# One VectorE addition moved ahead of a product of a later unit, and the last half tile given a PSUM bank and an output buffer of its own

## The chip, the cores and the metric

The kernel runs on one core of a Trainium2 chip. The metric is the device time of one execution in microseconds (us). The runs of the kernel before lie within 0.7% of each other; what is compared below is the median of several runs, and one execution recorded by the hardware profiler.

Engines are named as the profile names them: PE (TensorE matmuls), PEld (TensorE weight loads), DVE (VectorE), ACT (ScalarE), POOL (GpSimd), SP (the engine that issues many of the transfers). A "q" behind an engine name is that engine's sequencer issuing a DMA or waiting.

## The reference

Linear attention with a decaying state (per batch and head a 48x48 state), then a multiplicative feed-forward block. B=4 batches, H=8 heads, S=768 steps, D=48; 3072 tokens of 384 features, d_ff=1024.

```python
def _attn_ref(r, k, v, w, u):
    state = zeros((B, H, D, D)); y = zeros_like(r)
    for t in range(S):
        kt, vt, rt, wt = k[:, :, t], v[:, :, t], r[:, :, t], w[:, :, t]
        cur = einsum('bhd,bhe->bhde', u[None] * kt, vt)
        y[:, :, t] = einsum('bhd,bhde->bhe', rt, state + cur)
        state = wt[:, :, :, None] * state + einsum('bhd,bhe->bhde', kt, vt)
    return y

def _moe_ref(x, w1, w2, w3, w_out):      # x: y as [3072, 384]
    a = x @ w1
    b = x @ w2
    return (a * b @ w3) @ w_out
```

All inputs and the output are float32; inside, the matmul operands are bf16.

## The kernel before

**Tiles.** The 768 steps are cut into 6 chunks of C=128. A *unit* is one chunk of one or two batches; there are 13 (`UNITS`: chunk, first batch, number of batches). From unit 3 on each has two batches, so its tiles are 128 time steps by 768 values (two batches, 8 heads, 48 features).

**One unit t, attention part.** `ln_t` takes the logarithm of the decay on ACT; `cs_t` forms its running sum with a triangular matmul into two PSUM banks; `e_t`, `ne_t`, `pc_t` (ACT) take exponentials of that sum. `KRk_t`, `rw_t`, `KRr_t` scale k and r; DMA transposes on SP (`dtk_t`, `dtr_t`; PE transposes in early units) turn them. `m_t_b` are the score matmuls, which are masked (`msk` on DVE, or `mcp` on ACT with `maff` on POOL or DVE). `ys_t` and `yi_t_b` sum the state's part and the chunk's own part of y in PSUM. The diagonal term with u goes beside it: `rk_t` (r times k), `ruk_t` (times u), `dg_t` (sum over a head), `dv_t` (times v). `yb_t` (L627) adds the PSUM y and `dv_t` into a bf16 tile in SBUF, on DVE. Unit 7 then transposes that tile on PE (`yt_7`, L646) and copies it to `xT` (`xT_7`, L650); units 6 and 8 to 12 do this by DMA transposes (`dty_t_b`, L636).

**One unit t, feed-forward part** (`block`). `a_t_g` and `b_t_g` (L727) are the two products x w1 and x w2 in 4 groups, `asb_t_g` copies a to SBUF on ACT, `abT_t_g` multiplies it with b out of PSUM on DVE. `o_t_b` (L748) multiplies with w34, the product of w3 and w_out that was formed earlier, eight matmuls for a tile of 128 tokens by 384 columns; `osb_t_b` (L753) copies the bank to an output buffer and `st_t_b` (L757) stores it. The tile (11, 0) is the last one (`LAST`); it is computed in two halves of 192 columns, `o_11_0` and `oh_11_0`, with two copies (`osb_11_0` on DVE, `osbh_11_0` on ACT) and two stores (`st_11_0` from SP, `sth_11_0` from ACT).

**What sets the order.** Each step registers a function under its name; `ORDER` is one long list of `step@engine` that is issued in this order, so every engine works through its own steps in the order of the list. PSUM has 8 banks; `BANKS` gives by name which bank (or pair) a step uses, and which of a few SBUF buffers (`so11_0=1` is output buffer 1 for tile (11, 0)). `one(key)` is the view of a bank. Waits are derived from these: a step that writes a bank waits for the last reader of that bank, and a reader waits for the last write to the bank that is issued ahead of it. So `cs10=3,4` and `y7=3,4` say that `cs_10` on PE has to wait until `yb_7` has read the y of unit 7 out of banks 3 and 4.

`rk` and the other work tiles are doubled (`N_A = 2`), so unit 10 uses the buffer that unit 8 used. The loads of r, k, v and w are issued from POOL and SP far ahead; late units land in tiles that held weights (`w_bf`, `wo_bf` in the profile's names).

Of the kernel before, what the change touches and what calls it, by code (L numbers as in the profile page):

```python
# [59 lines left out]
a10_3=6 b10_3=1 sa10_3=2 o10_0=1 so10_0=3 o10_1=1 so10_1=1 cs11=0,1 m11_0=4,5 M11_0=1 m11_1=0,1 M11_1=3 y11=2,3  # L60
a11_0=5 b11_0=4 sa11_0=1 a11_1=4 b11_1=1 sa11_1=1 a11_2=2 b11_2=6 sa11_2=2 a11_3=0 b11_3=7 sa11_3=0 o11_0=2 so11_0=1
o11_1=3 so11_1=0 cs12=5,6 m12_0=5,6 M12_0=0 m12_1=0,1 M12_1=2 y12=1,2 a12_0=5 b12_0=7 sa12_0=0 a12_1=1 b12_1=4
sa12_1=1 a12_2=3 b12_2=2 sa12_2=2 a12_3=6 b12_3=5 sa12_3=2 o12_0=4 so12_0=3 o12_1=0 so12_1=2
"""
ORDER = """
table@ACT zeros@DVE mask1@DVE win_0@POOL kin_0@SP ones@DVE win_2@POOL rin_0@SP u@SP padkr@DVE padr@DVE vin_0@SP
# [36 lines left out]
asb_5_3@ACT b_5_1@PE S_7@POOL osb_4_0@ACT abT_5_3@DVE m_7_0@PE st_4_0@SP ys_7@PE ruk_7@POOL mcp_7_0@ACT m_7_1@PE  # L103
abT_5_1@DVE st_2_1@SP kv_8@PE msk_7_1@DVE st_2_0@SP a_6_2@PE dtk_8@SP cs_9@PE maff_7_0@POOL dg_7@DVE b_6_0@PE ne_9@ACT
dtr_8@SP T_8@DVE a_6_0@PE asb_6_2@ACT KRk_9@DVE e_9@ACT yi_7_0@PE a_6_3@PE rw_9@DVE dtk_9@SP dv_7@DVE asb_6_0@ACT
yi_7_1@PE o_4_1@PE ln_10@ACT rk_10@DVE win_11@SP yb_7@DVE KRr_9@POOL o_5_0@PE osb_4_1@ACT dg_8@DVE Sb_7@ACT pc_9@ACT
asb_6_3@ACT cs_10@PE rk_9@DVE dtr_9@SP yt_7@PE ruk_9@POOL e_10@ACT o_5_1@PE xT_7@DVE st_4_1@SP osb_5_0@DVE pc_10@ACT
ne_10@ACT abT_6_0@DVE b_6_2@PE dv_8@POOL iw_10@ACT osb_5_1@DVE b_6_3@PE abT_6_2@DVE st_5_1@SP ln_12@ACT m_8_0@PE
abT_6_3@DVE m_8_1@PE rin_12@POOL ys_8@PE mcp_8_1@ACT a_7_2@PE dg_9@DVE a_6_1@PE rin_11@POOL asb_7_2@ACT msk_8_0@DVE
# [28 lines left out]
def kernel(  # L138
# [13 lines left out]
    nc = tc.nc  # L152
    B, H, S, D = r.shape
    C = 128
# [16 lines left out]
    def many(n, shape, dt, name):  # L171
        return [sb.tile(shape, dt, name=f"{name}_{i}", tag=f"{name}_{i}") for i in range(n)]
# [28 lines left out]
    osb = many(N_OSB, [P, DM], F32, "osb")  # L201
# [25 lines left out]
    bank = {}  # L227
    for e in BANKS.split():
        key, _, at = e.partition("=")
# [3 lines left out]
    def op(name):  # L233
        def keep(fn):
            assert name not in steps, name
            steps[name] = fn
            return fn
        return keep

    def copier(eng):  # L240
        return {"ACT": nc.scalar.copy, "DVE": nc.vector.tensor_copy, "POOL": nc.gpsimd.tensor_copy}[eng]
# [4 lines left out]
    def one(key):  # L246
        return banks[:, bank[key], :]
# [74 lines left out]
    QUEUE = {"SP": nc.sync, "POOL": nc.gpsimd, "ACT": nc.scalar}  # L322
# [26 lines left out]
    for h in range(N_W12):  # L349
        f = slice(h * (DFF // N_W12), (h + 1) * (DFF // N_W12))  # L350
# [13 lines left out]
    for h in range(N_W3):  # L364
        f = slice(h * FI // N_W3, (h + 1) * FI // N_W3)
# [345 lines left out]
    def block(t):  # L711
        c, b0, nb = UNITS[t]
        T = nb * C
        per = 512 // T
        x, ab = xT[t % N_X], abT[t % N_AB]
        for g in range(FI // per):
            def gv(z):
                return one(f"{z}{t}_{g}").rearrange("p (f t) -> p f t", t=T)

            for z, wt in (("a", w1_bf), ("b", w2_bf)):  # L720
                @op(f"{z}_{t}_{g}")
                def _(eng, z=z, wt=wt, g=g, gv=gv):
                    o = one(f"{z}{t}_{g}").rearrange("p (f t) -> p f t", t=T)
                    for f in range(per):
                        fi = g * per + f
                        for di in range(DI):
                            nc.tensor.matmul(o[:, f, :], lhsT=wt[:, di, fi * P:(fi + 1) * P], rhs=x[:, di, :T],  # L727
                                             start=(di == 0), stop=(di == DI - 1))

            @op(f"asb_{t}_{g}")  # L730
            def _(eng, g=g):
                copier(eng)(a_sb[bank[f"sa{t}_{g}"]], one(f"a{t}_{g}"))  # L732

            @op(f"abT_{t}_{g}")
            def _(eng, g=g):
                sa = a_sb[bank[f"sa{t}_{g}"]]
                nc.vector.tensor_mul(ab[:, g * per:(g + 1) * per, :T], sa.rearrange("p (f t) -> p f t", t=T),  # L737
                                     one(f"b{t}_{g}").rearrange("p (f t) -> p f t", t=T))
        for b in range(nb):
            row = (b0 + b) * S + c * C  # L740
            parts = 2 if (t, b) == LAST else 1
            for z, mark in enumerate(("", "h")[:parts]):
                cols = slice(z * DM // parts, (z + 1) * DM // parts)

                @op(f"o{mark}_{t}_{b}")
                def _(eng, b=b, cols=cols):
                    for fi in range(FI):
                        nc.tensor.matmul(one(f"o{t}_{b}")[:, cols], lhsT=ab[:, fi, b * C:(b + 1) * C],  # L748
                                         rhs=w34[:, fi, cols], start=(fi == 0), stop=(fi == FI - 1))

                @op(f"osb{mark}_{t}_{b}")
                def _(eng, b=b, cols=cols):
                    copier(eng)(osb[bank[f"so{t}_{b}"]][:, cols], one(f"o{t}_{b}")[:, cols])  # L753

                @op(f"st{mark}_{t}_{b}")
                def _(eng, row=row, b=b, cols=cols):
                    QUEUE[eng].dma_start(out[row:row + C, cols], osb[bank[f"so{t}_{b}"]][:, cols])  # L757

    for fi in range(FI):
        w34_block(fi)  # L760
# [6 lines left out]
    with tc.manual_schedule():  # L767
        for e in ORDER.split():
            name, _, eng = e.partition("@")
# [37 lines left out]
```

## Time and profile before

| | |
|---|---|
| median of 3 runs | 164.16 us (163.75, 164.16, 164.83) |
| profiled execution, its own time | 163.85 us |
| its span | 162.1 us (1.75 us lie around it) |
| mean granted TensorE clock | 0.997 |
| PE / DVE / ACT / POOL busy | 153.5 / 125.4 / 96.9 / 103.2 us |
| DMA | 25.83 MB in 103,718 packets |

The span runs from the first to the last recorded instruction. A row of the timeline gives start, duration, engine, line, operation, output and inputs, shapes, and how many instructions are merged in it; in square brackets stands how long the engine sat idle before and what released it. The starts of instructions that follow each other on DVE or ACT lie some 0.08 us ahead of the end of the one before, and those of matmuls some 0.16 us: durations include the pipeline. So the pace of a chain of matmuls is read from start to start.

### The profile page before, as it was taken

The numbers are of one execution on the slowest core, as the hardware profiler recorded it, in microseconds if no ns is written. First come the engines' busy times: TensorE is split into PE (matmuls) and PEld (weight loads), VectorE is DVE, ScalarE is ACT, GpSimd is POOL, SyncE is SP. The second block draws the span as 40 slices with busy tenths as digits, with TensorE's granted clock in tenths as the row PEclk, the third lists the DMA queues.
The fourth block names the chain that finished last, engine by engine and source line by source line (L and its number), as shares of the span: only waits on it lengthen the run. The fifth ranks groups of instructions, "written<-read, shape, count | busy, mean of one in ns | idle before, by whom it ended". The sixth has DMA issues, their size and how long they took to land.

```text
span 162.1 us, 4606 instructions
## 1 busy us (share of the span) xinstructions
PE 153.5 (95%) x1923; PEld 117.3 (72%) x1923; DVE 125.4 (77%) x201; ACT 96.9 (60%) x161; POOL 103.2 (64%) x96
## 2 busy tenths in 40 slices
PE   6878899999999999999999989999999999999991
PEld 2336489977767699678887858877778678988760
DVE  6299977728997899999888999999696964566600
ACT  3157842575299598784988759579456544433230
POOL 7997996855268798799697539978628673000000
PEclk9999999999999999999999999999999999999998
DMA  6999999999999999999999997999998925132042
GB/s 111 222 159 180 196 195 242 209 170 215 219 155 161 177 259 167 137 120 172 147 186 169 230 202 195 94 142 132 184 174 182 201 28 146 28 121 97 6 146 97
DMA packets 103718, 25.83 MB, mean 159 GB/s; under 512 B 95825, under 2 KB 101713, under 8 KB 103697
## 3 DMA queue, kind: packets, MB, share of 16 engines
q0 software_dynamic: 76096, 15.18, 115.3%
q1 hardware_dynamic: 27456, 10.26, 30.5%
q8 instruction: 15, 0.25, 0.7%
q10 hardware_dynamic: 144, 0.10, 0.2%
q14 instruction: 7, 0.05, 0.1%
HBM read 27.98 MB, written 4.72 MB: 202 GB/s over the span
## 4 chain that ended last, share of the span: by engine, by line
PE 62%; DMA 20%; POOL 6%; DVE 6%; issue 2%; SPq 1%; ACT 0%; DVEq 0%; POOLq 0%
PE banks L727 31%; PE banks L748 18%; DMA rin<-in_r_dram 9%; DMA w_bf<-in_moe_w_dram 8%; DMA u_f<-in_u_dram 4%; PE banks L564 3%; PE banks L609 2%; PE banks L437 1%; PE banks L680 1%; PE banks L599 1%; PE banks L525 1%; POOL w_bf L358 1%; DVE dg L543 1%; POOL win L343 1%; POOL kin L343 1%
## 5 line engine op out<-in xcount | busy, mean ns | idle before, releaser
L727 PE MATMUL banks<-xT,w_bf 128*128 128x256 bf16 (+1 forms) x624 | 68.6, 264 | 0.0
L727 PEld LDWEIGHTS <-w_bf 128*128 128x128 bf16 x624 | 55.5, 98 | 7.0
L737 DVE TENSOR_TENSOR abT<-a_sb,banks 128x512 bf16<-128x512 f32 x48 | 31.9, 683 | 17.1 <-ACT a_sb L732 9.6
L732 ACT COPY a_sb<-banks 128x512 f32<-128x512 f32 x48 | 27.6, 591 | 21.5 <-PE banks L727 14.7
L748 PE MATMUL banks<-w,abT 128*128 128x384 bf16 (+1 forms) x200 | 33.9, 320 | 0.0
L748 PEld LDWEIGHTS <-abT 128*128 128x128 bf16 x200 | 18.8, 98 | 10.4
L583 DVE TENSOR_TENSOR Mbf<-banks,mask 128x1024 bf16<-128x1024 f32 x14 | 16.9, 1216 | 0.8 <-PE banks L564 0.6
L753 ACT COPY osb<-banks 128x384 f32<-128x384 f32 (+1 forms) x18 | 8.5, 471 | 13.6 <-PE banks L748 11.8
L421 ACT ACTIVATE lw<-win 128x768 bf16<-128x768 f32 (+1 forms) x13 | 10.3, 799 | 10.3 <-DMA win<-in_w_dram 10.3
L343 POOL DMA_DIRECT2D win<-in_w_dram x11 | 12.5, 1140 | 2.8 <-DMA wo_bf<-in_moe_w_out_dram 1.3
L537 POOL TENSOR_TENSOR ruk<-rk,u_bc 128x768 bf16<-128x768 bf16 (+1 forms) x7 | 10.8, 1537 | 4.9 <-DVE rk L533 4.4
L627 DVE TENSOR_TENSOR yb<-banks,dv 128x768 bf16<-128x768 f32 (+1 forms) x13 | 11.6, 892 | 2.4 <-PE banks L609 1.7
L570 ACT CAST Mbf<-banks 128x1024 bf16<-128x1024 f32 x10 | 10.0, 1014 | 4.6 <-PE banks L564 4.5
L454 ACT ACTIVATE NEt<-banks 128x768 bf16<-128x768 f32 (+1 forms) x13 | 9.9, 768 | 3.8 <-PE banks L437 2.7
L343 POOL DMA_DIRECT2D kin<-in_k_dram x8 | 9.1, 1143 | 4.5 <-issue 3.2
L543 DVE TENSOR_REDUCE dg<-ruk 128x16 f32<-128x768 bf16 (+1 forms) x13 | 11.5, 881 | 0.1
L316 PE MATMUL banks<-zeros 128*128 128x512 bf16 x35 | 10.0, 428 | 1.3 <-DVE zeros L257 1.3
L343 POOL DMA_DIRECT2D rin<-in_r_dram x8 | 9.1, 1142 | 2.3 <-PE banks L564 1.4
L343 POOL DMA_DIRECT2D vin<-in_v_dram x8 | 9.1, 1140 | 0.4 <-DMA rin<-in_r_dram 0.4
L564 PE MATMUL banks<-KRT 64*128 64x128 bf16 x192 | 8.1, 217 | 0.4 <-ACT KRT L529 0.3
L609 PEld LDWEIGHTS <-Mbf 128*128 128x128 bf16 x192 | 6.8, 96 | 1.9 <-DVE Mbf L583 0.7
L564 PEld LDWEIGHTS <-KRT 64*128 64x128 bf16 x192 | 5.5, 94 | 3.4 <-issue 1.1
(103 smaller groups left out, 243.6 us busy)
## 6 DMA issues: line engine op xcount, KB each, us to landing
out_dram<-osb SPq DMA_DIRECT2D x23, 192.0 KB, 2.3
win<-in_w_dram POOLq DMA_DIRECT2D x9, 384.0 KB, 10.1
w_bf<-in_moe_w_dram POOLq DMA_DIRECT2D x4, 512.0 KB, 12.6
w_bf<-in_moe_w_dram POOLq DMA_DIRECT2D x4, 384.0 KB, 8.3
rin<-in_r_dram POOLq DMA_DIRECT2D x7, 192.0 KB, 10.1
kin<-in_k_dram POOLq DMA_DIRECT2D x7, 192.0 KB, 10.0
vin<-in_v_dram POOLq DMA_DIRECT2D x7, 192.0 KB, 9.1
wo_bf<-in_moe_w_out_dram POOLq DMA_DIRECT2D x1, 768.0 KB, 11.3
```

The source lines that it names most:

```text
L343: QUEUE[eng].dma_start(dst, src)
L421: nc.scalar.activation(LW[:, :, :D], ww, Act.Ln)
L537: vec(eng).tensor_mul(ruks.rearrange("t (b h) d -> t b (h d)", b=nb), rks.rearrange("t (b h) d -> t b (h d)", b=nb), u_bc[:, None, :].to_b ...
L543: nc.vector.reduce_sum(dgs, ruks, axis=AX.X)
L564: nc.tensor.matmul(o[:, e, q, :], lhsT=KRTs[a:a + PAD, 0, b * HP + q, :], rhs=KRTs[a:a + PAD, 1, b * HP + q, :], start=True, stop=True)
L583: nc.vector.tensor_mul(Mbf[bank[f"M{t}_{b}"]], mview(), mask.rearrange("s (j q) t -> s j q t", j=2))
L609: nc.tensor.matmul(o[:, h % 2, b, h // 2, :], lhsT=M[:, h % 2, h // 2, :], rhs=vv[:, b * H + h, :], start=(not c and b == 0 and h < 2), st ...
L627: nc.vector.tensor_add(ybs.rearrange("t b (q e d) -> t e (b q) d", e=2, d=D), yview().rearrange("t e (x d) -> t e x d", d=D), dvs.rearrang ...
L727: nc.tensor.matmul(o[:, f, :], lhsT=wt[:, di, fi * P:(fi + 1) * P], rhs=x[:, di, :T], start=(di == 0), stop=(di == DI - 1))
L732: copier(eng)(a_sb[bank[f"sa{t}_{g}"]], one(f"a{t}_{g}"))
L737: nc.vector.tensor_mul(ab[:, g * per:(g + 1) * per, :T], sa.rearrange("p (f t) -> p f t", t=T), one(f"b{t}_{g}").rearrange("p (f t) -> p f ...
L748: nc.tensor.matmul(one(f"o{t}_{b}")[:, cols], lhsT=ab[:, fi, b * C:(b + 1) * C], rhs=w34[:, fi, cols], start=(fi == 0), stop=(fi == FI - 1))
```

## The change

Two edits. In `ORDER`, `yb_7@DVE` and `rk_10@DVE` change places (`win_11@SP`, a load of w for unit 11, stands between them and keeps its place on SP). In `block`, the second half of the last tile gets keys of its own, `oh11_0` for the bank and `soh11_0` for the output buffer: PSUM bank 6 in place of bank 2, and output buffer 0 in place of buffer 1. Engines, instructions, shapes and the number of instructions stay the same.

```diff
-sa12_1=1 a12_2=3 b12_2=2 ... o12_0=4 so12_0=3 o12_1=0 so12_1=2
+sa12_1=1 a12_2=3 b12_2=2 ... o12_0=4 so12_0=3 o12_1=0 so12_1=2 oh11_0=6 soh11_0=0
...
-yi_7_1@PE o_4_1@PE ln_10@ACT rk_10@DVE win_11@SP yb_7@DVE KRr_9@POOL o_5_0@PE ...
+yi_7_1@PE o_4_1@PE ln_10@ACT yb_7@DVE win_11@SP rk_10@DVE KRr_9@POOL o_5_0@PE ...
...
                 @op(f"o{mark}_{t}_{b}")
-                def _(eng, b=b, cols=cols):
+                def _(eng, b=b, cols=cols, mark=mark):
                     for fi in range(FI):
-                        nc.tensor.matmul(one(f"o{t}_{b}")[:, cols], lhsT=ab[:, fi, b * C:(b + 1) * C],
+                        nc.tensor.matmul(one(f"o{mark}{t}_{b}")[:, cols], lhsT=ab[:, fi, b * C:(b + 1) * C],
...
                 @op(f"osb{mark}_{t}_{b}")
-                    copier(eng)(osb[bank[f"so{t}_{b}"]][:, cols], one(f"o{t}_{b}")[:, cols])
+                    copier(eng)(osb[bank[f"so{mark}{t}_{b}"]][:, cols], one(f"o{mark}{t}_{b}")[:, cols])
...
                 @op(f"st{mark}_{t}_{b}")
-                    QUEUE[eng].dma_start(out[row:row + C, cols], osb[bank[f"so{t}_{b}"]][:, cols])
+                    QUEUE[eng].dma_start(out[row:row + C, cols], osb[bank[f"so{mark}{t}_{b}"]][:, cols])
```

On DVE, in the stretch where units 7 to 10 overlap, the instructions stand like this; `yb_111` is the y tile of odd units (here `yb_7`), `rk_102` the r k tile of even units (here `rk_10`), `dv_109` the diagonal term of unit 7, `dg_106` that of unit 8, and the last row is `rk_9`. The names in square brackets are the counters that the instruction waits for (DMASW: a load from POOL).

```order
 L491 TENSOR_TENSOR rw_87<-w_bf,iw_85 128x768 [waits DMASW6_49]
 L552 TENSOR_TENSOR dv_109<-vin_73,dg_107 128x768 [waits DMASW5_49,DVE_49]
+L627 TENSOR_TENSOR yb_111<-banks,dv_109 128x2x8x48 [waits DVE_49,PE_49]
 L533 TENSOR_TENSOR rk_102<-w_bf 128x768 [waits DMASW6_49,DMASW0_49]
-L627 TENSOR_TENSOR yb_111<-banks,dv_109 128x2x8x48 [waits DVE_49,PE_49]
 L543 TENSOR_REDUCE dg_106<-ruk_104 128x16
 L533 TENSOR_TENSOR rk_103<-w_bf 128x768
```

The addition moved up by one place, directly behind the product `dv_7` that it reads; nothing else on DVE moved.

On ACT, at the very end of the program, the copies of the last output tiles stand like this; `osb_137` to `osb_140` are the output buffers 0 to 3, the 128x192 rows are `osbh_11_0` and its store `sth_11_0`.

```order
 L753 COPY osb_140<-banks 128x384 [waits DMAHW6_49,DVE_49,PE_49]
 L753 COPY osb_139<-banks 128x384 [waits DMAHW7_49,PE_49]
-L753 COPY osb_138<-banks 128x192 [waits DMAHW0_49,DVE_49]
-L757 DMA out_dram<-osb_138 128x192 [waits Activation_49]
+L753 COPY osb_137<-banks 128x192 [waits DMAHW1_49,PE_49,Activation_49]
+L757 DMA out_dram<-osb_137 128x192 [waits Activation_49]
```

The last copy no longer waits for a DVE instruction but for PE, and for the store that last read output buffer 0 (DMAHW1). On PE the first matmul of `oh_11_0` now waits for ACT, the last reader of bank 6 (`asb_12_3`); on POOL and SP nothing moved.

More of the change, by code (lines that the diff above doesn't have):

```diff
@@ L62 @@
 o11_1=3 so11_1=0 cs12=5,6 m12_0=5,6 M12_0=0 m12_1=0,1 M12_1=2 y12=1,2 a12_0=5 b12_0=7 sa12_0=0 a12_1=1 b12_1=4
-sa12_1=1 a12_2=3 b12_2=2 sa12_2=2 a12_3=6 b12_3=5 sa12_3=2 o12_0=4 so12_0=3 o12_1=0 so12_1=2
+sa12_1=1 a12_2=3 b12_2=2 sa12_2=2 a12_3=6 b12_3=5 sa12_3=2 o12_0=4 so12_0=3 o12_1=0 so12_1=2 oh11_0=6 soh11_0=0
 """
@@ L105 @@
 dtr_8@SP T_8@DVE a_6_0@PE asb_6_2@ACT KRk_9@DVE e_9@ACT yi_7_0@PE a_6_3@PE rw_9@DVE dtk_9@SP dv_7@DVE asb_6_0@ACT
-yi_7_1@PE o_4_1@PE ln_10@ACT rk_10@DVE win_11@SP yb_7@DVE KRr_9@POOL o_5_0@PE osb_4_1@ACT dg_8@DVE Sb_7@ACT pc_9@ACT
+yi_7_1@PE o_4_1@PE ln_10@ACT yb_7@DVE win_11@SP rk_10@DVE KRr_9@POOL o_5_0@PE osb_4_1@ACT dg_8@DVE Sb_7@ACT pc_9@ACT
 asb_6_3@ACT cs_10@PE rk_9@DVE dtr_9@SP yt_7@PE ruk_9@POOL e_10@ACT o_5_1@PE xT_7@DVE st_4_1@SP osb_5_0@DVE pc_10@ACT
@@ L745, in _ @@
                 @op(f"o{mark}_{t}_{b}")
-                def _(eng, b=b, cols=cols):
+                def _(eng, b=b, cols=cols, mark=mark):
                     for fi in range(FI):
-                        nc.tensor.matmul(one(f"o{t}_{b}")[:, cols], lhsT=ab[:, fi, b * C:(b + 1) * C],
+                        nc.tensor.matmul(one(f"o{mark}{t}_{b}")[:, cols], lhsT=ab[:, fi, b * C:(b + 1) * C],
                                          rhs=w34[:, fi, cols], start=(fi == 0), stop=(fi == FI - 1))
                 @op(f"osb{mark}_{t}_{b}")
-                def _(eng, b=b, cols=cols):
-                    copier(eng)(osb[bank[f"so{t}_{b}"]][:, cols], one(f"o{t}_{b}")[:, cols])
+                def _(eng, b=b, cols=cols, mark=mark):
+                    copier(eng)(osb[bank[f"so{mark}{t}_{b}"]][:, cols], one(f"o{mark}{t}_{b}")[:, cols])
                 @op(f"st{mark}_{t}_{b}")
-                def _(eng, row=row, b=b, cols=cols):
-                    QUEUE[eng].dma_start(out[row:row + C, cols], osb[bank[f"so{t}_{b}"]][:, cols])
+                def _(eng, row=row, b=b, cols=cols, mark=mark):
+                    QUEUE[eng].dma_start(out[row:row + C, cols], osb[bank[f"so{mark}{t}_{b}"]][:, cols])
     for fi in range(FI):
```

## The prediction

> **What bounds the kernel now.** I read first the page's busy times and its chain of waits, to see which engine sets the end.
>
> ```profile
> span 162.1 us, 4606 instructions
> PE 153.5 (95%) x1923; PEld 117.3 (72%) x1923; DVE 125.4 (77%) x201; ACT 96.9 (60%) x161; POOL 103.2 (64%) x96
> PE 62%; DMA 20%; POOL 6%; DVE 6%; issue 2%; SPq 1%; ACT 0%; DVEq 0%; POOLq 0%
> ```
>
> PE carries the chain, but 95% is an average. The busy time by stretch shows where PE still has gaps, and PE's own waits between 95.8 and 158.6 us show who makes them.
>
> ```profile
> core 0: us, PE busy (x) PEld busy (x) DVE busy (x) ACT busy (x) POOL busy (x), PEclk, DMA share, GB/s
> 95.90:126.00 30.10, 30.10 (x385) 24.01 (x386) 26.59 (x41) 20.07 (x32) 21.66 (x17) 1.00 1.48 159
> 126.00:158.60 32.60, 32.59 (x341) 25.51 (x339) 18.20 (x27) 12.76 (x21) 6.71 (x6) 1.00 0.44 94
> 158.60:162.10 3.50, 0.00 (x0) 0.00 (x0) 0.36 (x1) 0.32 (x1) 0.00 (x0) 0.88 0.34 112
> PE banks L437 <- DVE yb L627: 0.6, 1, 0.6
> PEld L437 <- DVE yb L627: 1.0, 1, 1.0
> ```
>
> From 95.9 to 158.6 us PE has no gap at all, at full clock; then come 3.5 us in which PE has nothing left. The only wait of PE in this part is for a `yb` at its beginning. So a microsecond saved there moves all later matmuls, as long as nothing else becomes late; and the tail adds directly to the time. The two edits touch just these two places, and I work them out apart.
>
> **Edit 1: `yb_7` ahead of `rk_10`.** PE's timeline at the gap:
>
> ```profile
> 92.50 2.76 PE L748 MATMUL banks<-w,abT 128*128 128x384 bf16 x16
> 95.89 0.50 PE L437 MATMUL banks<-lw,LT 128*128 128x384 bf16 x2 [0.62 <-DVE yb L627]
> 96.43 0.49 PE L646 MATMUL banks<-I,yb 128*128 128x128 bf16 x6
> 96.76 1.46 PE L748 MATMUL banks<-w,abT 128*128 128x384 bf16 x8
> 98.06 0.71 PE L727 MATMUL banks<-xT,w_bf 128*128 128x256 bf16 x5
> ```
>
> The first row is `o_4_1` and `o_5_0`, the second `cs_10`, then `yt_7`, `o_5_1`, `b_6_2`. Eight matmuls of L748 take 1.30 us from start to start (96.76 to 98.06), so sixteen from 92.50 end their turn at 95.10. `cs_10` started at 95.89: the gap is **0.79 us** by this pace (0.62 by the row, which counts the pipeline's tail as busy). `cs_10` writes banks 3 and 4, which `yb_7` reads. On DVE and POOL:
>
> ```profile
> 92.10 0.95 DVE L552 TENSOR_TENSOR dv<-vin,dg 128x768 bf16<-128x768 bf16 x1
> 92.97 2.00 DVE L533 TENSOR_TENSOR rk<-w_bf 128x768 bf16<-128x768 bf16 x1
> 94.89 0.94 DVE L627 TENSOR_TENSOR yb<-banks,dv 128x768 bf16<-128x768 f32 x1
> 95.75 0.94 DVE L543 TENSOR_REDUCE dg<-ruk 128x16 f32<-128x768 bf16 x1
> 96.61 0.54 DVE L533 TENSOR_TENSOR rk<-w_bf 128x768 bf16<-128x768 bf16 x1
> 98.60 0.55 DVE L753 COPY osb<-banks 128x384 f32<-128x384 f32 x1
> 92.39 2.15 POOL L499 TENSOR_TENSOR KR<-rw,Et 128x768 bf16<-128x768 bf16 x1 [1.90 <-ACT Et L495]
> ```
>
> `rk_10` took 2.00 us, while the same product at 96.61 took 0.54. What is different is POOL: `KRr_9` ran until 92.39 + 2.15 = 94.54, and `rk_10` ended at 94.97, 0.43 later, as if it had begun when POOL was done. Is that a rule of this kernel? I looked for other pairs.
>
> ```profile
> 83.12 1.15 DVE L491 TENSOR_TENSOR rw<-w_bf,iw 128x768 bf16<-128x768 bf16 x1
> 83.03 0.82 POOL L702 TENSOR_TENSOR Sst<-Tst,pc 128x384 f32<-128x384 f32 x1
> 105.13 0.95 DVE L627 TENSOR_TENSOR yb<-banks,dv 128x768 bf16<-128x768 f32 x1
> 105.35 1.63 POOL L499 TENSOR_TENSOR KR<-rw,Et 128x768 bf16<-128x768 bf16 x1 [0.39 <-issue]
> 75.01 0.96 DVE L627 TENSOR_TENSOR yb<-banks,dv 128x768 bf16<-128x768 f32 x1 [0.23 <-PE banks L609]
> 75.53 1.49 POOL L552 TENSOR_TENSOR dv<-vin,dg 128x768 bf16<-128x768 bf16 x1
> ```
>
> The product of two SBUF tiles at 83.12 also ended 0.42 us behind POOL's (84.27 against 83.85). But a `yb`, whose first input is in PSUM, takes 0.95 us beside a POOL product (105.13, 75.01), and POOL's are not stretched by it either (1.63 and 1.49). So I take it that `rk` is held by POOL and `yb` is not.
>
> The Trainium skill's page "SBUF — State Buffer", section "SBUF: two separate sides", says that VectorE and GpSimd share one pair of ports as an exclusive lock for a whole instruction, and that VectorE needs it in a two-port mode or with two SBUF inputs. The rows above agree, for both kinds. By the page `yb_7`, with one SBUF input, leaves `KRr_9` alone, and the sum below stands; had one such input been enough for the lock, the third rival's time would come out.
>
> Then the new order gives: `yb_7` starts when `dv_7`, which it reads, is through (92.10 + 0.95 = 93.05), ends at about 94.0; `rk_10` starts behind it, waits for POOL as before, and still ends at about 94.97. `rk_10` pays nothing for its move, since it only loses time that it spent waiting; its reader `ruk_10` stands 14 places behind it on DVE. If the cover were gone (`KRr_9` at 1.63 us as in the row at 105.35, done at 94.0) `rk_10` would end at 94.5, earlier still. DVE goes on with `dg_8` at 94.89 in place of 95.75, **0.86 us** earlier, and with it `rk_9`, `xT_7` and the copy at 98.60.
>
> PE can now start `cs_10` at 95.10, a full microsecond after `yb_7` ended: 0.79 us gained. What is late next? `yt_7` would start at 95.64 and writes bank 2, which ACT must have copied out:
>
> ```profile
> 94.90 0.59 ACT L732 COPY a_sb<-banks 128x512 f32<-128x512 f32 x1
> ```
>
> That ends at 95.49: a margin of 0.15 us. `xT_7` wants `rk_9` out of the way (0.86 earlier) and `yt_7` (0.79 earlier): both come. `m_8_0` needs bank 6, copied out by the row at 98.60, which moves by more than PE does. From here on every engine hands on to the next, so they move together; only what is tied to DMA could stay behind. The closest such place is unit 8's transposes (`dty_8`), with PE beside it:
>
> ```profile
> L636 SPq DMA_TRANSPOSE xT<-yb x2: 1190/1218/1246, 106.1 to 107.3; - x2
> DMA to landing us min/median/max: 4.5/4.9/5.3
> 111.62 2.34 PE L727 MATMUL banks<-xT,w_bf 128*128 128x256 bf16 x20
> 58.52 0.66 PE banks L727 x6
> L636 SPq DMA_TRANSPOSE xT<-yb x12: 1179/1248/2288, 78.2 to 140.6; - x12
> DMA to landing us min/median/max: 2.3/4.7/6.2
> ```
>
> The second transpose is issued at 107.35 and lands 4.5 us later, at 111.86; `a_8_0`, its first reader, follows six matmuls behind 111.62, at 112.28. The margin is 0.4 us. The first transpose follows `yb_8` (105.13 + 0.95) at once, so its issue moves with DVE and PE, by 0.79. I cost this at nothing; if the landing did not move at all, PE would wait 0.79 - 0.42 = 0.37 us and keep 0.42. If it took the 6.2 us of the longest, PE would wait 1.3 us.
>
> **Edit 2: the tail.** The end of the program by the timeline:
>
> ```profile
> 156.79 1.81 PE L748 MATMUL banks<-w,abT 128*128 128x384 bf16 x18
> 158.63 0.36 DVE L753 COPY osb<-banks 128x192 f32<-128x192 f32 x1 [4.66 <-PE banks L748]
> 159.03 0.32 ACT L753 COPY osb<-banks 128x192 f32<-128x192 f32 x1 [1.23 <-DVE osb L753]
> 159.37 0.37 ACTq L757 DMA_DIRECT2D out_dram<-osb  x1
> out_dram<-osb ACTq DMA_DIRECT2D x1, 96.0 KB, 1.7
> out_dram<-osb SPq DMA_DIRECT2D x4, 192.0 KB, 1.9
> ```
>
> PE's last matmul ends at 158.60. Although `o_11_0` was done eight matmuls earlier, its DVE copy starts only at 158.63, since both halves lie in one bank; and the ACT copy of the other half waits for DVE's. Then come the store's issue at 159.37 and 1.7 us to its landing. With a bank of its own the DVE copy goes beside `oh_11_0`, and the ACT copy starts where DVE's did: 159.03 - 158.63 = **0.40 us** gained. The new waits cost nothing that I can find. Bank 6 was last read by `asb_12_3`, without which PE could not have begun `o_12_0`, 24 matmuls ahead. Output buffer 0 was last stored by `st_11_1`, issued when `o_11_1` was copied; from there to PE's end lie two whole tiles and two halves, 2 x 1.30 + 2 x 0.66 = 3.9 us, and a store lands after 1.9 us (last row). Nothing stands behind the ACT copy but its own store. On SP, `st_11_0` now goes out some 0.66 us earlier, into a queue with nothing behind it. Bounds of this term: 0 (if the copy waited for something else) and 0.40.
>
> **The sum**, against the profiled execution: 163.85 - 0.79 - 0.40 = 162.66 us. The median of the runs shown is 0.31 above that execution, so I expect 164.16 - 1.19 = 162.97, **163.0 us**, 0.7% less. All rivals are told on that base. Differences within 1% (1.64 us) are about what a measurement of this kernel cannot tell from no change, so my forecast itself falls there.
>
> **Rivals.**
> - *The first gain is eaten by the transposes.* For it: a margin of 0.4 us, and landings that scatter between 2.3 and 6.2 us. Against it: issue and competing loads move along. With landings that stay where they are PE keeps 0.42, so 163.3; at 1.2 us later than now it keeps nothing, 163.8.
> - *Slower: the same transposes land much later.* Where they take the longest seen, 6.2 in place of 4.5 us, `a_8_0` waits 1.3 us: 164.16 - 1.19 + 1.3 = 164.3, slower than before. It decides from 1.6 us later on; over 1% slower would need 3.2 us, which no transpose here came near.
> - *`yb_7` holds POOL back.* `KRr_9` needed 2.15 us where its like needs 1.63: it seems to have waited 0.5 us at its start, behind `dv_7`. If `yb_7` went ahead of it too, it would end 0.95 us later, `rk_10` at 95.9, and the copy at 98.60 would come 0.1 us later than now and end at 99.25. `m_8_0` on PE, which needs its bank, stood twelve matmuls (1.3 us) behind 98.06, at about 99.4: PE would give back all but some 0.1 us: 163.7. The rows at 75.01 and 105.13 speak against it.
> - *The change does not do what it says*: `cs_10` waits for something else that is late as well. But PE's waits name `yb` alone, and `ln_10`, its input, stands on ACT ahead of the copy at 94.90. 163.8, with the tail alone.
>
> **How the numbers follow.** Forecast 0.62; gain eaten (163.3 to 163.8) 0.17; slower by the transposes 0.06; POOL held back 0.06; no effect at `cs_10` 0.05; the remaining 0.04 for what I do not see. The runs before spread over 1.1 us, so a median may be off by some 0.4 us either way. The range from 162.2 to 164.1 holds the forecast with that spread, and the rivals up to 163.8; 164.3 stays out. Faster by over 1% needs 0.45 us more than the sum, which only the spread gives: 0.18. Slower by over 1%: 0.05. Within 1%: 0.77.
>
> **What would show it.** In the new profile: `yb` at about 93.1 with 0.95 us, `rk_10` behind it still ending at about 95.0; `cs_10` at 95.1 without the wait for `yb`; PE without gaps until about 157.8; the ACT half copy 0.03 us behind PE's last matmul, and a span near 160.9. A PE wait at L727 for a transpose near 111.5 would mean the first rival; a `KRr_9` over 3 us the third. I would be wrong most simply if the matmuls do not run back to back once everything comes 0.8 us earlier.

## The result, and the profile after

| | before | after |
|---|---|---|
| median | 164.16 us (19 runs, 163.39 to 165.35) | 163.0 us (19 runs, 162.42 to 164.28) |
| ratio, 95% interval | | 0.9925 [0.9906, 0.9943] |
| profiled execution | 163.85 us | 164.28 us |
| start of `kv_3` on PE in it | 52.43 | 54.06 |
| from there to PE's last end | 106.17 | 105.37 |
| from PE's last end to the end of the span | 3.50 | 3.14 |

The change is faster by 0.75% with an interval clear of zero: about 1.2 us, as forecast. The profile of the changed kernel must be read with care, though: its execution is the slowest of the 19, even slower than the profiled one of before. The chain of waits says where that comes from: one piece of it (start, duration, what) and PE's row of `kv_3` and `kv_4`, first of before, then of after.

```profile
36.72 13.93 DMA rin<-in_r_dram
52.43 0.69 PE L680 MATMUL banks<-vin,KR 128*64 128x48 bf16 x32
```

```profile
36.70 15.58 DMA rin<-in_r_dram
54.06 0.69 PE L680 MATMUL banks<-vin,KR 128*64 128x48 bf16 x32
```

A load of r for unit 4, issued at the same time in both, landed 1.6 us later, and `kv_3` (L680), which starts 1.78 us behind that landing in both, started 1.63 us late; the work behind it runs late by as much. Neither edit lies ahead of that point. So the starts below are read against it: 1.63 is to be taken off. One of the profiles further down, of the kernel with `KRr_9` on DVE, is from a disturbed execution too (167.14 us, its median 163.74); durations at one place are read from it, and one late transfer, which speaks for that execution alone.

DVE and POOL of after, where the additions and products stand (start, duration, what):

```profile
93.72 0.95 DVE L552 TENSOR_TENSOR dv<-vin,dg 128x768 bf16<-128x768 bf16 x1
94.78 0.96 DVE L627 TENSOR_TENSOR yb<-banks,dv 128x768 bf16<-128x768 f32 x1
95.65 0.94 DVE L533 TENSOR_TENSOR rk<-w_bf 128x768 bf16<-128x768 bf16 x1
96.51 0.94 DVE L543 TENSOR_REDUCE dg<-ruk 128x16 f32<-128x768 bf16 x1
94.02 2.15 POOL L499 TENSOR_TENSOR KR<-rw,Et 128x768 bf16<-128x768 bf16 x1 [1.90 <-ACT Et L495]
```

`yb_7` begins 0.11 us after `dv_7` is through and is not stretched beside POOL. `KRr_9` takes 2.15 us, as before: `yb_7` did not hold it back. `rk_10` now overlaps POOL for only half a microsecond, takes 0.94 us in place of 2.00, and ends at 96.59, 0.42 behind POOL's end, as before (95.0 when 1.63 is taken off). PE at the same place, and its busy time from there on:

```profile
94.13 2.76 PE L748 MATMUL banks<-w,abT 128*128 128x384 bf16 x16
96.72 0.49 PE L437 MATMUL banks<-lw,LT 128*128 128x384 bf16 x2
95.30:158.20 62.90, 62.90 (x722) 49.41 (x721) 46.20 (x69) 33.85 (x57) 29.23 (x23) 1.00 0.98 127
```

`cs_10` starts 2.59 us behind `o_4_1` (3.39 before), the pace of sixteen matmuls, with no wait; and PE is busy for 62.90 of the 62.90 us from 95.30 to 158.20. Unit 8's two transposes, the closest place behind it that hangs on a DMA (the first row ends with their issues, 106.9 and 108.2):

```profile
L636 SPq DMA_TRANSPOSE xT<-yb x2: 1188/1218/1247, 106.9 to 108.2; - x2
DMA to landing us min/median/max: 4.2/4.6/5.0
```

The tail:

```profile
158.80 0.36 DVE L753 COPY osb<-banks 128x192 f32<-128x192 f32 x1 [4.00 <-PE banks L748]
159.51 0.32 ACT L753 COPY osb<-banks 128x192 f32<-128x192 f32 x1 [0.89 <-PE banks L748]
159.85 0.37 ACTq L757 DMA_DIRECT2D out_dram<-osb  x1
```

PE's last matmul ends at 159.43. The DVE copy begins 0.62 us ahead of that, the ACT copy 0.08 behind it (0.43 before).

### The profile page after: what moved, and what is told of

It reads as the page before. It is cut to its first block, busy times and chain, and to the rows that moved or that the text cites. A ratio compares the mean times of both kernels' runs of the same rounds, so it can differ in the third digit from the quotient of the medians.

```text
span 162.6 us, 4604 instructions
## 1 busy us (share of the span) xinstructions
PE 154.0 (95%) x1921; PEld 117.7 (72%) x1923; DVE 124.6 (77%) x201; ACT 97.1 (60%) x161; POOL 103.2 (63%) x96
## 4 chain that ended last, share of the span: by engine, by line
PE 65%; DMA 23%; POOL 6%; issue 2%; ACT 1%; DVE 1%; POOLq 0%; ACTq 0%
PE banks L727 33%; PE banks L748 19%; DMA rin<-in_r_dram 10%; DMA w_bf<-in_moe_w_dram 8%; DMA win<-in_w_dram 5%; PE banks L564 3%; PE banks L609 2%; POOL win L343 2%; POOL kin L343 2%; PE banks L437 1%; PE banks L680 1%; PE banks L599 1%; PE banks L525 1%; POOL rin L343 1%; POOL Mbf L578 1%
## 5 line engine op out<-in xcount | busy, mean ns | idle before, releaser
L727 PE MATMUL banks<-xT,w_bf 128*128 128x256 bf16 (+1 forms) x624 | 68.6, 264 | 0.0
L727 PEld LDWEIGHTS <-w_bf 128*128 128x128 bf16 x624 | 55.5, 98 | 7.0
L316 PE MATMUL banks<-zeros 128*128 128x512 bf16 x33 | 10.6, 462 | 1.3 <-DVE zeros L257 1.2
```

What stands on the lines that cost most here:

```text
L316: nc.tensor.matmul(banks[:, at, :], lhsT=zeros[:, :C], rhs=zeros, start=True, stop=True)
```

## The experiments

The explanation to be tested: two edits, each at its own place, that add up; POOL holds `rk` and not `yb`; PE has no gap behind `cs_10`, so what is saved there stays. Beside the timed ratio, two stretches of each profile are read, since the landing of r at 50 us moves whole executions by more than the effect: from the start of `kv_3` to PE's last end, and from there to the end of the span. Each ratio is against executions of the kernel before that were taken with it; the two stretches are of one profile each.

| kernel | ratio to before, 95% interval | `kv_3` to PE's end | PE's end to the end |
|---|---|---|---|
| before | | 106.17 | 3.50 |
| after | 0.9925 [0.9906, 0.9943] | 105.37 | 3.14 |
| order alone | 0.9960 [0.9946, 0.9975] | 105.36 | 3.49 |
| tail alone | 0.9974 [0.9958, 0.9990] | 106.15 | 3.13 |
| bank alone (one execution) | | 106.16 | 3.11 |
| `yb_7` later still | 1.0065 [1.0041, 1.0089] | 107.02 | 3.51 |
| after, `rk_10` behind `dg_8` | 0.9937 [0.9912, 0.9962] | 105.37 | 3.13 |
| `KRr_9` on DVE, old order | 0.9948 [0.9921, 0.9975] | not read | |
| after, `dv_7` early (one execution) | | 106.00 | 3.15 |
| after, last tile 288 + 96 | 0.9937 [0.9913, 0.9961] | 105.37 | 3.18 |

**The order alone**

```diff
-... ln_10@ACT rk_10@DVE win_11@SP yb_7@DVE KRr_9@POOL ...
+... ln_10@ACT yb_7@DVE win_11@SP rk_10@DVE KRr_9@POOL ...
```

> Only yb_7 and rk_10 change places. Theory (the two edits act apart, each at its own place): PE's 0.79 us gap ahead of cs_10 goes and nothing gives it back, so the time falls by 0.79 us against the kernel before (ratio 0.995); in the profile cs_10 follows o_5_0 without a wait, rk_10 ends when it did relative to KRr_9 (0.43 us behind POOL's end), and the tail still has the DVE copy behind PE's end and the ACT copy 0.40 us behind that. Rival (the order brings less, because part of it is given back later, and the tail carries the gain): under 0.4 us less, with a PE wait of some 0.4 us at a later L727 row.

```profile
93.23 2.76 PE L748 MATMUL banks<-w,abT 128*128 128x384 bf16 x16
95.83 0.49 PE L437 MATMUL banks<-lw,LT 128*128 128x384 bf16 x2
```

0.66 us less by the ratio (0.41 to 0.89), 0.81 in the first stretch and nothing beyond 0.01 in the second. `cs_10` follows `o_4_1` by 2.60 us, and from 90 us on PE has no wait, at `cs_10` or at L727: nothing was given back. The tail is the old one, the DVE copy 0.04 and the ACT copy 0.43 behind PE's end (158.53):

```profile
158.57 0.36 DVE L753 COPY osb<-banks 128x192 f32<-128x192 f32 x1 [4.66 <-PE banks L748]
158.96 0.32 ACT L753 COPY osb<-banks 128x192 f32<-128x192 f32 x1 [1.24 <-DVE osb L753]
```

**The tail alone**

The edits of `BANKS` and `block` stay as in the change; the order goes back to the old one. Against the changed kernel:

```diff
-... ln_10@ACT yb_7@DVE win_11@SP rk_10@DVE KRr_9@POOL ...
+... ln_10@ACT rk_10@DVE win_11@SP yb_7@DVE KRr_9@POOL ...
```

> Only the last half tile gets its own bank and buffer; rk_10 stays ahead of yb_7. Theory: PE's gap at cs_10 stays at 0.79 us by the pace (0.62 by the wait row), the ACT half copy starts within 0.1 us of PE's last matmul in place of 0.44, so the time falls by 0.35 to 0.40 us (ratio 0.998). Rival (the order carries all of the change): no difference, with the end of the program waiting for the other store in place of the ACT copy.

0.43 us less by the ratio (0.16 to 0.69), 0.37 in the second stretch, 0.02 in the first. Its wait at `cs_10` is still there, and the ACT copy starts 0.08 behind PE's end (158.43):

```profile
PE banks L437 <- DVE yb L627: 0.6, 1, 0.6
158.51 0.32 ACT L753 COPY osb<-banks 128x192 f32<-128x192 f32 x1 [0.89 <-PE banks L748]
```

The two stretches of the edits add up to those of both: 0.81 + 0.37 = 1.18 us against 0.80 + 0.36 = 1.16.

**The bank alone, the output buffer shared**

Against the kernel with the tail alone:

```diff
-... oh11_0=6 soh11_0=0
+... oh11_0=6 soh11_0=1
```

> As the tail edit alone, but the half tile keeps output buffer 1 and gets only its own bank. Theory (the shared bank made both copies wait): the DVE copy runs beside the last eight matmuls, the ACT copy starts within 0.1 us of PE's last matmul, as with both. Rival (the shared buffer made the second copy wait): the ACT copy starts 0.4 us behind PE's last matmul, as before. One look, read from the profile's last rows and not from the time.

```profile
158.70 0.36 DVE L753 COPY osb<-banks 128x192 f32<-128x192 f32 x1 [4.00 <-PE banks L748]
159.36 0.32 ACT L753 COPY osb<-banks 128x192 f32<-128x192 f32 x1 [0.84 <-PE banks L748]
```

With PE's end at 159.32 the ACT copy starts 0.04 behind it. In this one execution the bank is the whole of the gain (3.11 us behind PE's end, against 3.13); a buffer of its own adds nothing, and the copy even starts 0.04 later with it. With it the copy also waits for ACT's own earlier copy into buffer 0 and for that buffer's last store; whether one of these is the reason was not tried.

**The addition later still**

```diff
-... ln_10@ACT rk_10@DVE win_11@SP yb_7@DVE KRr_9@POOL o_5_0@PE osb_4_1@ACT dg_8@DVE ...
+... ln_10@ACT rk_10@DVE win_11@SP KRr_9@POOL o_5_0@PE osb_4_1@ACT dg_8@DVE yb_7@DVE ...
```

> The opposite of the order edit: yb_7 goes one place further back, behind dg_8, on the kernel before. Theory (PE waits for yb_7 at cs_10 and for nothing else there, and no later slack takes it up): yb_7 starts 0.86 us later, the wait row at cs_10 grows from 0.62 to about 1.48 us, and the time grows by 0.86 us against the kernel before (ratio 1.005). Rival (later slack takes up a delay): cs_10 late by as much, but the time within 0.3 us of before, with fewer or shorter waits elsewhere on PE.

```profile
97.05 0.50 PE L437 MATMUL banks<-lw,LT 128*128 128x384 bf16 x2 [1.48 <-DVE yb L627]
```

The wait is 1.48 us in place of 0.62, and the first stretch 0.85 longer; by the ratio 0.67 to 1.46 us slower. A delay at `cs_10` goes to the end one for one, and so did the gain.

**`rk_10` behind `dg_8`, on the changed kernel**

```diff
-... yb_7@DVE win_11@SP rk_10@DVE KRr_9@POOL o_5_0@PE osb_4_1@ACT dg_8@DVE ...
+... yb_7@DVE win_11@SP KRr_9@POOL o_5_0@PE osb_4_1@ACT dg_8@DVE rk_10@DVE ...
```

> The changed kernel with rk_10 one place further back, behind dg_8. Theory (rk_10 is held while KRr_9 runs on POOL, yb and dg are not): dg_8 starts right behind yb_7, rk_10 then starts when KRr_9 is done or nearly so and takes 0.55 us to at most 0.7 us in place of 0.94; rk_9 comes some 0.4 us earlier. PE has no gap there any more, so the time is that of the changed kernel (ratio 0.9925 to before, within 0.2%). Rival (rk_10 is slow by itself, through its data): it takes 0.94 to 2.0 us there too. Second rival (DVE still bounds some later wait): the time falls by another 0.4 us.

```profile
93.16 2.15 POOL L499 TENSOR_TENSOR KR<-rw,Et 128x768 bf16<-128x768 bf16 x1 [1.90 <-ACT Et L495]
94.79 0.94 DVE L543 TENSOR_REDUCE dg<-ruk 128x16 f32<-128x768 bf16 x1
95.65 1.02 DVE L533 TENSOR_TENSOR rk<-w_bf 128x768 bf16<-128x768 bf16 x2
97.00 0.56 DVE L650 COPY xT<-banks 128x768 bf16<-128x768 bf16 x1 [0.33 <-PE banks L646]
```

`dg_8`, a reduction with one SBUF input, runs beside POOL without a stretch; `rk_10` and `rk_9` (the row with x2) take 0.55 us each once POOL is done at 95.31. DVE then waits 0.33 us for PE's `yt_7`: the 0.4 us that it gains are idle time, since DVE bounds nothing here. The first stretch is that of after (105.37), and the ratios' intervals overlap.

**`KRr_9` on DVE, the old order**

```diff
-... ln_10@ACT rk_10@DVE win_11@SP yb_7@DVE KRr_9@POOL ...
+... ln_10@ACT rk_10@DVE win_11@SP yb_7@DVE KRr_9@DVE ...
```

> The kernel before, with rk_10 ahead of yb_7 as before and the old tail, but KRr_9 computed on DVE behind yb_7 in place of POOL. Theory (POOL held rk_10): rk_10 takes 0.55 us, yb_7 starts some 1.45 us earlier relative to dv_7, cs_10 has no wait, and the time falls by about 0.79 us (ratio 0.995) although the order is the old one. Rival (rk_10 took 2.0 us because of its data or its waits for loads): it takes 2.0 us still, cs_10 waits as before, and the time is that of before or, with 0.55 us more work on DVE, up to 0.5 us more.

```profile
94.15 0.55 DVE L533 TENSOR_TENSOR rk<-w_bf 128x768 bf16<-128x768 bf16 x1
94.62 0.95 DVE L627 TENSOR_TENSOR yb<-banks,dv 128x768 bf16<-128x768 f32 x1
95.49 0.55 DVE L499 TENSOR_TENSOR KR<-rw,Et 128x768 bf16<-128x768 bf16 x1
```

With POOL's product gone, `rk_10` takes 0.55 us at its old place with its old data, and the time falls by 0.41 to 1.30 us without the order edit. So the 2.00 us were POOL's doing. In this profile PE also waits for a late transpose, as in the rival to which I had given the sign "slower":

```profile
124.67 2.78 PE L727 MATMUL banks<-xT,w_bf 128*128 128x256 bf16 x24 [1.91 <-DMA xT<-yb]
DMA to landing us min/median/max: 5.9/6.9/8.0
```

The second row is of unit 9's two transposes, issued at 115.0 and 116.5. The later landed 8.0 us after its issue, longer than any in the profile before, and PE waited 1.91 us at `a_9_2`. So such a wait can occur; but this is the one profiled execution of the twelve, of a kernel other than the changed one, and the other eleven (162.69 to 164.28 us) were not profiled. How often it occurs, and whether moving `KRr_9` has to do with it, is not shown.

**`dv_7` early, on the changed kernel**

```diff
-... dg_7@DVE b_6_0@PE ... dtk_9@SP dv_7@DVE asb_6_0@ACT ...
+... dg_7@DVE dv_7@DVE b_6_0@PE ... dtk_9@SP asb_6_0@ACT ...
```

> The changed kernel with dv_7 moved up behind dg_7, so that no product of two SBUF tiles with a row-wise factor stands on DVE when KRr_9 starts on POOL. Theory (KRr_9's 2.15 us are 0.52 us of waiting behind dv_7): KRr_9 takes 1.63 us, rk_10 ends 0.4 us behind its end. Rival (KRr_9 was slowed by rk_10 or yb_7 beside it): it takes 2.15 us still. One look, read from the durations.

```profile
94.70 1.64 POOL L499 TENSOR_TENSOR KR<-rw,Et 128x768 bf16<-128x768 bf16 x1 [2.81 <-ACT a_sb L732]
94.73 0.96 DVE L627 TENSOR_TENSOR yb<-banks,dv 128x768 bf16<-128x768 f32 x1 [0.17 <-PE banks L609]
95.60 1.15 DVE L533 TENSOR_TENSOR rk<-w_bf 128x768 bf16<-128x768 bf16 x1
PE banks L727 <- DVE Tst L687: 0.5, 1, 0.5
```

`KRr_9` takes 1.64 us with a `yb` beside it for 0.96 of them; `rk_10` ends at 96.75, 0.41 behind POOL's end (96.34). So the 0.52 us of before were waiting behind `dv_7`. Not expected: `T_8`, pushed back by `dv_7`, now makes PE wait 0.5 us at L727, and the first stretch is 0.64 longer than that of after.

**The last tile in 288 and 96 columns**

```diff
-cols = slice(z * DM // parts, (z + 1) * DM // parts)
+cut = [0, 288, DM] if parts == 2 else [0, DM]
+cols = slice(cut[z], cut[z + 1])
```

> The changed kernel with the last tile cut into 288 and 96 columns in place of 192 and 192. Theory (behind PE's last matmul the tail is the ACT copy, its store and its landing): PE's work stays the same, the last ACT copy falls from 0.32 to some 0.24 us, and the time by 0.1 us, less than a measurement can tell. Rival: matmuls of 96 columns run no faster than weights are loaded, PE ends up to 0.3 us later and the time grows by as much. Read from the span behind PE's last matmul.

```profile
158.20 0.46 DVE L754 COPY osb<-banks 128x288 f32<-128x288 f32 x1 [4.32 <-PE banks L749]
158.59 0.24 ACT L754 COPY osb<-banks 128x96 f32<-128x96 f32 x1 [0.89 <-PE banks L749]
out_dram<-osb ACTq DMA_DIRECT2D x1, 48.0 KB, 1.8
```

(Its lines are one higher.) PE is not slower with 96 columns, and the ACT copy falls to 0.24 us as expected, but the tail does not get shorter: 3.18 against 3.14 us. The 0.08 us that the copy saves are lost at the store, which lands after 1.8 us where that of 96 KB took 1.7. The two copies end 0.17 us apart here and 0.67 in after, so the two last stores run closer together; whether that or the smaller pieces hold the store up is not shown. The ratio is not apart from that of after. No kernel here beats the changed one.

## Why the prediction was right, point by point

- **What bounds the kernel.** Held. No PE gap behind `cs_10` in after, and a delay (a wait of 1.48 us in place of 0.62) as well as a gain went to the end in full.
- **The gap of 0.79 us.** Measured 0.80 with both edits and 0.81 alone, so by the pace and not by the 0.62 of the wait row. A wait row counts from the modelled end of the last matmul; here the start-to-start pace gave what could be won.
- **`rk_10` pays nothing for its move.** Held: same end, 0.42 us behind POOL. The cause is shown, not only argued, by the run with POOL's product on DVE (0.55 us at its old place) and by the one in which it starts once POOL is done (0.55 us too).
- **`yb` is not held and holds nothing.** Held: 0.96 us beside POOL, `KRr_9` at 2.15 with it and 1.64 once `dv_7` was out of the way. That closes the rival of POOL held back. By the Trainium skill's page "SBUF — State Buffer", section "SBUF: two separate sides", a VectorE instruction with two SBUF inputs needs the ports that it shares with GpSimd; the 2.00 us of `rk_10` (two) and the 0.96 us of `yb_7` (one) beside POOL agree.
- **What is late next.** The margin of 0.15 us at `yt_7` and of 0.4 us at unit 8's transposes sufficed in the profile of after, as PE has no wait there. The second of those transposes is issued 54.1 us behind `kv_3` (108.2 - 54.06), where before it was 54.9 (107.35 - 52.43): its issue moved with PE, as costed. The landings took 0.3 us less than before (4.2 and 5.0 against 4.5 and 5.3), so this profile doesn't test a late one. The rival of late transposes was named rightly, but at unit 8; the one profile in which PE did wait for a transpose has it at unit 9, and its landing of 8.0 us went beyond the 6.2 that I took as the longest.
- **The tail's 0.40 us.** The mechanism held; 0.36 us were measured. The term that was mis-sized is the start of the ACT copy: not "where DVE's did", 0.04 behind PE, but at 0.08. The run with the bank alone shows the 0.04.
- **The level.** 163.0 against 163.0. The step from the profiled execution to the median was sound for before; the profiled execution of after would have misled by 1.3 us, so its span of 162.6 in place of the 160.9 that I named says nothing of the edits. That the time is met to a tenth of a microsecond is in part luck: the interval of the ratio allows a gain of 0.94 to 1.54 us, and the median of the three runs before happens to be that of all nineteen, which spread over 2.0 us and not 1.1.

## What to carry to other kernels

Where one engine runs without a gap to the end, find its last wait and the tail behind it: here a saving there counted in full (0.80 and 0.36 us), while 0.4 us saved on DVE where PE did not wait for it brought nothing. Price a gap by the pace of starts on either side. When an instruction takes several times its usual time, look at what another engine runs beside it, and put in its place one whose operands don't need what is held; and when an execution moves by more than the effect, measure from a point behind the disturbance.

## What was not expected of the hardware

- The landing of one early load sets most of the scatter between the profiled executions: PE's start at `kv_3` lies between 52.3 and 54.1 us, and in all ten 1.78 or 1.79 us behind that landing. The load is issued between 36.3 and 38.1 us and takes 13.9 to 15.6 us. From `kv_3` to PE's end, executions of kernels with the same order agree within 0.02 us.
- A store of 48 KB landed no sooner than one of 96 KB (1.8 and 1.7 us), so cutting the last piece finer brought nothing in this kernel.
- A held product ends 0.41 to 0.43 us behind POOL's end although it takes 0.55 us alone: by that difference, an estimate, some 0.13 us of it lie ahead of the wait.
